# One run of probability-times-value matmuls for two head groups, and a table for the dense parts between score steps

## Chip, cores, metric

The kernel runs on one core of a Trainium2 chip. The metric is the device time of one execution in microseconds (us), as the median of several runs.

## What is computed

A parallel block on 2048 tokens of width 640: a layer norm, then sliding-window attention (32 heads of width 20, window 256) and a sigmoid-gated feed-forward of width 1536, both added to the input.

```python
scores = jnp.einsum("bhqd,bhkd->bhqk", q, k) * (Dh ** -0.5)
mask = (idx[:, None] - idx[None, :] >= 0) & (idx[:, None] - idx[None, :] < W)
p = _softmax(jnp.where(mask[None, None], scores, -1e9), axis=-1)
o = jnp.einsum("bhqk,bhkd->bhqd", p, v)
...
h = _sigmoid(g) * u                  # g = xn @ w_gate, u = xn @ w_up
xn = _layernorm(x, axis=-1)
return x + _A_ref(xn, A_wqkv, A_wo) + _B_ref(xn, B_w_gate, B_w_up, B_w_down)
```

## The kernel before, in words

The sequence is cut into four chunks c of 512 tokens. For each chunk the kernel makes the normalised, transposed input `xnT` (`g_norms`, `turn_block`), projects Q and K (`g_qk`, L292) and V (`g_v`, L318), computes gate and up (`g_gu`, L392 and L399) and at the end the down projection plus the output projection of attention (`g_out`, `down` L413, `add_wo` L420). These are the dense matmuls: 128 rows by 128 columns of weights against 512 or 320 moving columns. Each block of five of them accumulates in one of three PSUM buffers (`ps_d`) and is then read by ScalarE (the tanh of the gate, L395; the copies of K, L298, and of half of V, L325) or VectorE (`h`, L403; the copies of Q, L296, and of the other half of V; the sum with x, L424).

Q and K go through DRAM to be spread over 32-row strips: a block of Q or K is copied to `st`, stored to the scratch `sq` or `sk` (L300) and read back by `spread` (L307) into `qT` or `kT`, eight head groups of four heads each. All of these transfers are issued by SyncE (SP) in the order of the program. `spread` of Q is issued after the second K block of a chunk, `spread` of K after the first row block of V.

Attention goes in 76 steps: 16 in chunk 0 and 20 in each of the chunks 1 to 3. A step (`scores`) does 16 to 32 small matmuls (L459; 20 rows by 64 columns of weights, several in different parts of the array at once), which fill the single score buffer `ps` of four PSUM banks. ScalarE takes the exponential of all of it into a probability tile `pT` (L464, 2048 columns), and GpSimd masks parts of that (L467, up to three selects). In chunk 0 a step belongs to one head group; later a pair of groups takes five steps: two "wide" steps of the first group, one "full" step with the unmasked key blocks of both, and two wide steps of the second group.

`pv` multiplies the probabilities by V for one group (L491; 128 rows by 32 columns of weights, four heads in four column strips), accumulates in the one buffer of `ps_a` and is followed by a transpose on VectorE (L501) and, deferred to `fill.behind`, the division by the row sum (L509, L513) and a transpose to `oc` (L517). It is called two steps after the group's last score step, directly ahead of that later step's scores.

The order on TensorE is written by the recording loop (L663 to L688): for each step, first the due `pv`, then `scores`, then dense parts from a queue of generators (`Fill`), each giving the nanoseconds of TensorE that a part stands for (`MM` = 216 for a 512-column matmul). How many is set by `fill.pull(credit)`: what is left of dense work ahead of a deadline, divided by the steps left. A part is a whole block of five matmuls, or a piece of the down projection. `fill.shut` keeps the output projection of a chunk back until its last `pv` is recorded. After the loop the last chunk's down and output projection follow, with the last group's `pv` in their midst (L707). Everything is in manual order: each engine executes its instructions as they are recorded.

Of the kernel before, what the change touches and what calls it, by code (L numbers as in the profile page):

```python
# [86 lines left out]
def steps_of(c):  # L87
    if c == 0:
        return [wide_step(g, r, False) for g in range(NG) for r in range(2)]
    out = []  # L90
    for g in range(0, NG, 2):
        out += [wide_step(g, 0, True), wide_step(g, 1, True), full_step((g, g + 1)),
                wide_step(g + 1, 0, True), wide_step(g + 1, 1, True)]
    return out


# [11 lines left out]
def kernel(  # L108
# [21 lines left out]
    lnp = pool("lnp", 4)  # L130
    xtp = pool("xtp", 2)
    stp = pool("stp", 5)
    qp = pool("qp", 2)
    kp = pool("kp", 3)
    vp = pool("vp", 10)
    hp = pool("hp", 14)
    pp = pool("pp", 4)
    op = pool("op", 7)
    onp = pool("onp", 2)
    tp = pool("tp", 1)  # L140
    np_ = pool("np", 1)
    ps_a = pool("ps_a", 1, space=bass.MemoryType.PSUM)
# [142 lines left out]
    def proj_block(w, c, m):  # L285


        base = 0 if w == "q" else D
        ps = ps_d.tile([P, CW], FP32, name="pqk", tag="d")
        for d in range(DC):  # L290
            wt = wqkv[:, d, base:base + D].rearrange("p (k m) -> p m k", m=DC)
            nc.tensor.matmul(ps, lhsT=wt[:, m, :], rhs=xnT[c][:, d, :],  # L292
                             start=(d == 0), stop=(d == DC - 1))
        st = stp.tile([P, CW], BF16, name="st")
        if w == "q":
            nc.vector.tensor_copy(out=st, in_=ps)  # L296
        else:
            nc.scalar.copy(out=st, in_=ps)  # L298
        dst = scratch[w, c % 2].rearrange("(h j) s -> h j s", j=32)
        nc.sync.dma_start(out=dst[:, 4 * m:4 * m + 4, :], in_=st)  # L300

    def spread(w, c, g0, g1):

        if g0 == 0:
            qk[w, c] = (qp if w == "q" else kp).tile([P, NG, CW], BF16, name=w + "T")
        src = scratch[w, c % 2].rearrange("(g p) s -> p g s", p=P)
        nc.sync.dma_start(out=qk[w, c][:, g0:g1, :], in_=src[:, g0:g1, :])  # L307

    def new_v(c, s):
        v = vp.tile([P, H * VW + 11], BF16, name="v")  # L310
# [45 lines left out]
    def g_qk(c):  # L356
        for w in "qk":
            for m in range(DC):
                proj_block(w, c, m)
                if c == 0 and w == "q" and m == 1:  # L360
                    load_x(1)
                if w == "k" and m == 1:
                    spread("q", c, 0, NG if c else 2)
                yield 5 * MM
        if c == 0:
            spread("k", c, 0, 1)
            spread("k", c, 1, 3)
            spread("q", c, 2, 4)
            spread("k", c, 3, 4)

    def g_v(c):
        for s in range(SBC):
            new_v(c, s)
            for hf in range(2):
                proj_v(c, s, hf, nc.scalar.copy if hf else nc.vector.tensor_copy)
            if s == 0:
                spread("k", c, 0, 2)
                spread("k", c, 2, NG)
            yield 10 * 136


    ht = {}
# [5 lines left out]
    def g_gu(c, f0, f1):  # L388
        for f in range(f0, f1):
            pg = ps_d.tile([P, CW], FP32, name="pg", tag="d")  # L390
            for d in range(DC):
                nc.tensor.matmul(pg, lhsT=part(wg, d, f), rhs=xnT[c][:, d, :],  # L392
                                 start=(d == 0), stop=(d == DC - 1))
            th = tp.tile([P, CW], FP32, name="th")
            nc.scalar.activation(out=th, in_=pg, func=TANH, scale=0.5)  # L395
            yield 5 * MM
            pu = ps_d.tile([P, CW], FP32, name="pu", tag="d")
            for d in range(DC):
                nc.tensor.matmul(pu, lhsT=part(wu, d, f), rhs=xnT[c][:, d, :],  # L399
                                 start=(d == 0), stop=(d == DC - 1))  # L400
            h = hp.tile([P, CW], BF16, name="h")
            ht[c, f] = h
            nc.vector.scalar_tensor_tensor(out=h, in0=th, scalar=1.0, in1=pu, op0=ADD, op1=MULT)  # L403
            yield 5 * MM


    oc = {}
# [44 lines left out]
    def scores(c, step):  # L452
        pt = pp.tile([P, HG, PTW], BF16, name="pT")
        ps = ps_s.tile([P, HG, CW], FP32, name="ps")
        for g, hf, r, q, n, col in step["scores"]:
            kc, kb = divmod(c * SBC + r, SBC)
            key = kb * P + hf * U
            for i in range(HG):
                nc.tensor.matmul(  # L459
                    ps[hf * U:(hf + 1) * U, i, col * U:(col + n) * U],  # L460
                    lhsT=qk["k", kc][32 * i:32 * i + DH, g, key:key + U],
                    rhs=qk["q", c][32 * i:32 * i + DH, g, q * U:(q + n) * U],
                    start=True, stop=True)
        nc.scalar.activation(out=pt[:, :, 0:CW], in_=ps, func=EXP, scale=SCALE)  # L464

# [15 lines left out]
            keep(spans(step["diag"], 2, 2), spans(step["diag"], 2, 2), 2, P, 0, 1)  # L481
        return pt

    def pv(c, g, parts):
        acc = ps_a.tile([P, CW], FP32, name="acc")
        flat = [(pt, *piece[1:]) for step, pt in parts for piece in step["pv"] if piece[0] == g]
        for k, (pt, r, q, n, col) in enumerate(flat):
            v = vt[c * SBC + r]
            for i in range(HG):
                h = g * HG + i  # L490
                nc.tensor.matmul(  # L491
                    acc[32 * i:32 * i + 32, q * U:(q + n) * U],
                    lhsT=v[:, h * VW:h * VW + 32], rhs=pt[:, i, col * U:(col + n) * U],
                    start=(k == 0), stop=(k == len(flat) - 1), skip_group_check=True)
        finish_group(c, g, acc)

    on = {}

    def finish_group(c, g, acc):
        t1 = np_.tile([P, 16, 32], FP32, name="t1")  # L500
        nc.vector.transpose(out=t1.rearrange("p b r -> p (b r)"), in_=acc)  # L501
        if c < NCH - 1 or g < NG - 1:
            fill.behind.append(lambda: scale_group(c, g, t1))
        else:
            scale_group(c, g, t1)

    def scale_group(c, g, t1):
        rec = np_.tile([P, 16, 1], FP32, name="rec")
# [11 lines left out]
    class Fill:  # L520
        def __init__(self):
            self.parts = []
            self.behind = []
            self.done = set()
            self.shut = set()

        def add(self, label, gen, cost):
            self.parts.append([label, gen, cost])

        def left(self, label):  # L530

            ahead = itertools.takewhile(lambda p: p[0] != label, self.parts)
            return sum(max(p[2], 0) for p in ahead)

        def one(self):
            label, gen, _ = self.parts[0]
            try:
                cost = next(gen)
                if cost:
                    self.flush()  # L540
                self.parts[0][2] -= cost
                return cost
            except StopIteration:
                self.parts.pop(0)
                self.done.add(label)
                return 0
# [2 lines left out]
            while self.behind:  # L549
                self.behind.pop(0)()  # L550

        def pull(self, ns):
            while ns > 0 and self.parts and self.parts[0][0] not in self.shut:
                ns -= self.one()
            return ns

        def until(self, label):
            while label not in self.done and self.parts:
# [80 lines left out]
    norms2 = g_norms(2, True)  # L639
    fill.add("gu0a", g_gu(0, 0, 4), 4 * GU)  # L640
    fill.add("wd", later(load_wd), 0)
    fill.add("gu0b", mix(g_gu(0, 4, 12), g_norms(1, True), 1), 8 * GU)
    fill.add("x2", later(load_x, 2), 0)
    fill.add("wo_i", later(turn_wo), 0)
    fill.add("qk1", g_qk(1), 50 * MM)
    fill.add("v1", g_v(1), 40 * 136)
    fill.add("wo", later(load_wo), 0)
    fill.add("gu1a", mix(g_gu(1, 0, 2), norms2, 0, 2, False), 2 * GU)
    fill.add("out0", mix(g_out(0), norms2, 0, 2), OUT)
    fill.add("x3", later(load_x, 3), 0)  # L650
    fill.add("qk2", g_qk(2), 50 * MM)
    fill.add("v2", g_v(2), 40 * 136)
    fill.add("gu1b", mix(g_gu(1, 2, 12), g_norms(3, False), 10), 10 * GU)
    fill.add("out1", mix(g_out(1), g_turns(3), 1, 3), OUT)
    fill.add("qk3", g_qk(3), 50 * MM)
    fill.add("v3", g_v(3), 40 * 136)
# [5 lines left out]
    ends = {}  # L662
    for t, (c, _, step) in enumerate(todo):  # L663
        for piece in step["pv"]:
            ends[c, piece[0]] = t


    cuts = [(ends[n, NG - 1] + 2, f"out{n}") for n in range(NCH - 1)] + [(len(todo), None)]
    fill.pull(6 * 5 * MM)
    parts = {}  # L670
    credit = 0
    fill.shut = {"out0", "out1", "out2"}
    for t, (c, k, step) in enumerate(todo):
        if k == 0 and c > 0:
            fill.until(f"qk{c}")
        if k == 2 and c > 0:
            fill.until(f"v{c}")
        for group in [x for x in ends if ends[x] == t - 2]:
            fill.flush()
            pv(*group, parts.pop(group))  # L680
            if group[1] == NG - 1:
                fill.shut.discard(f"out{group[0]}")
        made = (step, scores(c, step))
        for g in dict.fromkeys(piece[0] for piece in step["pv"]):
            parts.setdefault((c, g), []).append(made)
        last, label = next(x for x in cuts if t < x[0])
        credit += fill.left(label) / (last - t)
        credit = fill.pull(credit)  # L688
    fill.pull(10 ** 9)
    fill.flush()  # L690

    c = NCH - 1
# [10 lines left out]
    for s in range(SBC):  # L703
# [1 line left out]
            ys[s, cut] = next(tiles)  # L705
            run(down(c, s, ys[s, cut], cut))
        if s == 1:  # L707
            pv(c, NG - 1, parts.pop((c, NG - 1)))

    s = SBC - 1  # L710
    cuts = (HALVES[0], (HALF, 4 * P), (4 * P, D))
# [40 lines left out]
```

The softmax here doesn't subtract the row's maximum and nothing guards it: scores larger than these inputs give would overflow.

## Time and profile before

| quantity | us |
|---|---|
| median of 5 runs | 315.88 (315.27 to 316.95) |
| the profiled execution, its own time | 316.95 |
| its span, first to last instruction | 315.2 |
| TensorE (PE) busy | 307.4 |
| ScalarE (ACT) busy | 193.2 |
| GpSimd (POOL) busy | 159.7 |
| VectorE (DVE) busy | 157.3 |
| transfers: 33.08 MB | 105 GB/s over the span |
| TensorE's granted clock | 1.000 |

The profile is of one execution. 1.75 us of its time lie around the span. In lines of the timeline, "xN" counts instructions that stand together, and the second number is from the start of the first to the modelled end of the last; the time that a group keeps TensorE is better read from its start to the start of the next group.

### The profile page before, as it was taken

How to read it: one execution, taken by the hardware profiler on the slowest of the kernel's cores; microseconds unless marked ns; L12 is line 12 of the kernel's file. 1: busy time of each engine (PE TensorE's matmuls, PEld its weight loads, DVE VectorE, ACT ScalarE, POOL GpSimd, SP SyncE). 2: the span in 40 equal slices, each digit the busy share in tenths (PEclk: the TensorE clock that was granted, in tenths of full speed). 3: DMA queues.
4: the chain of work that ended last, by engine and by line, in shares of the span. 5: the costliest groups of instructions: out<-in, count | busy, mean ns of one | idle time of the engine just before them, and what ended most of it. 6: DMA issues, size and time to landing. Idle time of an engine off the chain costs nothing.

```text
span 315.2 us, 10536 instructions
## 1 busy us (share of the span) xinstructions
PE 307.4 (98%) x4631; PEld 176.3 (56%) x4666; DVE 157.3 (50%) x313; ACT 193.2 (61%) x179; POOL 159.7 (51%) x257
## 2 busy tenths in 40 slices
PE   8899999999999999999999999999999999999996
PEld 3554444556566656644466656544456764444674
DVE  3541396663865563347953542544552433673234
ACT  4634686778765458677654457776765657777200
POOL 3000287766777537454954536355255656565300
DMA  7975999526733155600045025700000010000002
GB/s 250 374 248 186 351 376 170 212 75 202 205 72 70 44 173 167 204 4 0 2 42 90 23 88 141 231 2 2 3 2 23 23 44 2 4 2 2 1 2 83
DMA packets 34573, 33.08 MB, mean 105 GB/s; under 512 B 9920, under 2 KB 33984, under 8 KB 34496
## 3 DMA queue, kind: packets, MB, share of 16 engines
q1 hardware_dynamic: 34096, 32.14, 34.9%
q8 instruction: 36, 0.59, 0.8%
q10 hardware_dynamic: 432, 0.28, 0.3%
q14 instruction: 9, 0.07, 0.1%
HBM read 21.00 MB, written 10.26 MB: 99 GB/s over the span
## 4 chain that ended last, share of the span: by engine, by line
PE 94%; DMA 2%; ACT 1%; issue 1%; SPq 1%; DVE 0%; ACTq 0%
PE pg L392 16%; PE pu L399 16%; PE y L413 15%; PE pqk L292 14%; PE ps L459 9%; PE acc L491 8%; PE pv L318 7%; PE y L420 6%; DMA xc<-in_A_x_dram 2%; PE d L413 2%; PE d L420 1%; ACT pT L464 1%; PE acc L413 0%; SPq L178 0%; SPq L173 0%
## 5 line engine op out<-in xcount | busy, mean ns | idle before, releaser
L467 POOL TENSOR_SCALAR_AFFINE_SELECT pT<-pT 128x512 bf16<-128x512 bf16 (+2 forms) x192 | 145.5, 789 | 133.8 <-ACT pT L464 133.7
L464 ACT ACTIVATE pT<-ps 128x2048 bf16<-128x2048 f32 x76 | 142.7, 1877 | 63.7 <-PE ps L459 60.2
L403 DVE SCALAR_TENSOR_TENSOR h<-th,pu 128x512 bf16<-128x512 f32 x48 | 32.8, 684 | 53.8 <-PE pu L399 29.1
L392 PE MATMUL pg<-xnT,wg 128*128 128x512 bf16 x226 | 58.9, 380 | 0.7
L399 PE MATMUL pu<-xnT,wu 128*128 128x512 bf16 x228 | 58.0, 380 | 1.1 <-issue 0.8
L413 PE MATMUL y<-wd,h 128*128 128x320 bf16 (+1 forms) x348 | 50.2, 297 | 0.0
L292 PE MATMUL pqk<-xnT,wqkv 128*128 128x512 bf16 x191 | 45.6, 381 | 0.5
L413 PEld LDWEIGHTS <-h 128*128 128x128 bf16 x396 | 36.7, 98 | 14.3
L501 DVE STREAM_TRANSPOSE t<-acc 128x512 f32<-128x512 f32 x32 | 22.8, 713 | 34.3 <-PE acc L491 34.0
L395 ACT ACTIVATE th<-pg 128x512 f32<-128x512 f32 x48 | 28.6, 595 | 17.7 <-PE pg L392 13.1
L399 PEld LDWEIGHTS <-wu 128*128 128x128 bf16 x240 | 22.0, 98 | 25.6 <-issue 0.6
L392 PEld LDWEIGHTS <-wg 128*128 128x128 bf16 x240 | 22.0, 98 | 25.1 <-issue 0.4
L459 PE MATMUL ps<-qT,kT 20*64 20x128 bf16 (+4 forms) x1856 | 32.5, 239 | 0.1
L292 PEld LDWEIGHTS <-wqkv 128*128 128x128 bf16 x200 | 22.5, 119 | 18.0 <-issue 0.6
L459 PEld LDWEIGHTS <-kT 20*64 20x64 bf16 x1856 | 20.6, 103 | 19.1 <-issue 15.4
L424 DVE SCALAR_TENSOR_TENSOR xn<-y,xc 128x320 bf16<-128x320 f32 (+1 forms) x29 | 13.9, 484 | 29.6 <-PE y L420 29.4
L491 PEld LDWEIGHTS <-v 128*32 128x32 bf16 x1376 | 19.5, 97 | 13.6 <-issue 11.0
L491 PE MATMUL acc<-pT,v 128*32 128x64 bf16 (+3 forms) x1376 | 26.0, 223 | 0.0
L318 PE MATMUL pv<-wqkv,xnT 128*128 128x320 bf16 x160 | 23.9, 300 | 1.1 <-ACT xnT L273 1.0
L513 DVE TENSOR_TENSOR on<-t,rec 128x320 bf16<-128x320 f32 (+4 forms) x48 | 22.2, 463 | 1.1
L420 PE MATMUL y<-wo,oc 128*128 128x320 bf16 (+1 forms) x145 | 21.6, 297 | 0.1
L296 DVE CAST st<-pqk 128x512 bf16<-128x512 f32 x20 | 13.7, 691 | 12.2 <-PE pqk L292 12.2
(49 smaller groups left out, 153.3 us busy)
## 6 DMA issues: line engine op xcount, KB each, us to landing
qT<-sq SPq DMA_DIRECT2D x3, 1024.0 KB
sq<-st SPq DMA_DIRECT2D x20, 128.0 KB, 3.0
sk<-st SPq DMA_DIRECT2D x20, 128.0 KB, 3.6
out_dram<-xn SPq DMA_DIRECT2D x15, 160.0 KB, 1.8
kT<-sk SPq DMA_DIRECT2D x3, 768.0 KB, 4.9
wg<-in_B_w_gate_dram SPq DMA_DIRECT2D x2, 960.0 KB
wu<-in_B_w_up_dram SPq DMA_DIRECT2D x2, 960.0 KB
xc<-in_A_x_dram SPq DMA_DIRECT2D x3, 640.0 KB, 5.5
```

Source lines behind the costliest of these rows:

```text
L292: nc.tensor.matmul(ps, lhsT=wt[:, m, :], rhs=xnT[c][:, d, :], start=(d == 0), stop=(d == DC - 1))
L318: nc.tensor.matmul(ps[:, 0:HALF], lhsT=xnT[c][:, d, s * P:(s + 1) * P], rhs=wqkv[:, d, 2 * D + hf * HALF:2 * D + (hf + 1) * HALF], start=( ...
L392: nc.tensor.matmul(pg, lhsT=part(wg, d, f), rhs=xnT[c][:, d, :], start=(d == 0), stop=(d == DC - 1))
L395: nc.scalar.activation(out=th, in_=pg, func=TANH, scale=0.5)
L399: nc.tensor.matmul(pu, lhsT=part(wu, d, f), rhs=xnT[c][:, d, :], start=(d == 0), stop=(d == DC - 1))
L403: nc.vector.scalar_tensor_tensor(out=h, in0=th, scalar=1.0, in1=pu, op0=ADD, op1=MULT)
L413: nc.tensor.matmul(y[:, 0:cut[1] - cut[0]], lhsT=ht[c, f][:, s * P:(s + 1) * P], rhs=wd[:, f, cut[0]:cut[1]], start=(f == 0), stop=False)
L420: nc.tensor.matmul(y[:, 0:cut[1] - cut[0]], lhsT=oc[c, m][:, s * P:(s + 1) * P], rhs=wo[:, m, cut[0]:cut[1]], start=False, stop=(m == DC - 1))
L459: nc.tensor.matmul(ps[hf * U:(hf + 1) * U, i, col * U:(col + n) * U], lhsT=qk["k", kc][32 * i:32 * i + DH, g, key:key + U], rhs=qk["q", c] ...
L464: nc.scalar.activation(out=pt[:, :, 0:CW], in_=ps, func=EXP, scale=SCALE)
L467: nc.gpsimd.affine_select(out=out, in_=in_, pattern=[[0, HG], [0, n], [sign, width]], compare_op=GE, fill=0.0, base=base, channel_multipli ...
L491: nc.tensor.matmul(acc[32 * i:32 * i + 32, q * U:(q + n) * U], lhsT=v[:, h * VW:h * VW + 32], rhs=pt[:, i, col * U:(col + n) * U], start=( ...
```

## The change

Five things are changed together.

1. `pv` handles a pair of head groups in one run: the first group accumulates in a `ps_d` buffer, the second in `ps_a`. The first is transposed at once; its scaling, and the transpose and scaling of the second, go to `fill.behind`, which now gives one entry after each dense part instead of all at once. 32 runs of L491 become 16 (twice as long).
2. The full step of a pair moves from third to last of the five. `pv` comes two steps after the pair's last step in chunk 0, one step after it later (`LAG`), that is, directly after the dense parts behind the full step.
3. Five probability tiles instead of four (a pair's five tiles live until its `pv`); one `on` buffer instead of two.
4. `qT` is kept in half tiles of four groups: three of those instead of two whole ones, so that a chunk's Q comes in two transfers.
5. The dense blocks of `g_qk`, `g_v` and `g_gu` can be parted by a score step: after two matmuls of five, or after half of a row block of V. How many parts stand behind each step is given by the table `PARTS` in place of credit, deadlines and `shut`. The norms' places in the queue are adjusted to the smaller parts.

```diff
-        out += [wide_step(g, 0, True), wide_step(g, 1, True), full_step((g, g + 1)),
-                wide_step(g + 1, 0, True), wide_step(g + 1, 1, True)]
+        out += [wide_step(g, 0, True), wide_step(g, 1, True), wide_step(g + 1, 0, True),
+                wide_step(g + 1, 1, True), full_step((g, g + 1))]
...
-    qp = pool("qp", 2)
+    qp = pool("qp", 3)
-    pp = pool("pp", 4)
+    pp = pool("pp", 5)
-    onp = pool("onp", 2)
+    onp = pool("onp", 1)
...
+            if d == 1:
+                yield 2 * MM
...
-        nc.sync.dma_start(out=qk[w, c][:, g0:g1, :], in_=src[:, g0:g1, :])
+        nc.sync.dma_start(out=qk[w, c, half][:, first:first + g1 - g0, :], in_=src[:, g0:g1, :])
...
-                    spread("q", c, 0, NG if c else 2)
-                yield 5 * MM
+                    spread("q", c, 0, GH if c else 2)
+                    if c:
+                        spread("q", c, GH, NG)
+                yield 3 * MM
...
-    def pv(c, g, parts):
-        acc = ps_a.tile([P, CW], FP32, name="acc")
+    def pv(c, pair, parts):
+        accs = []
+        for g, home, tag in ((2 * pair, ps_d, "d"), (2 * pair + 1, ps_a, "acc")):
+            acc = home.tile([P, CW], FP32, name="acc", tag=tag)
...
+        first = turn_group(accs[0])
+        fill.behind += [lambda: scale_group(c, 2 * pair, first),
+                        lambda: scale_group(c, 2 * pair + 1, turn_group(accs[1]))]
...
-                if cost:
-                    self.flush()
+                if cost and self.behind:
+                    self.behind.pop(0)()
...
+        def take(self, n):
+            while n > 0 and self.parts:
+                n -= self.one() > 0
...
+    LAG = (2, 1, 1, 1)
+    PARTS = [
+        5, 4, 4, 7, 2, 4, 5, 4, 3, 4, 4, 4, 2, 5, 3, 5, 2, 4, 3, 4,
+        2, 5, 3, 6, 5, 3, 5, 7, 3, 3, 4, 10, 6, 6, 4, 4, 5, 3, 3, 3,
+        3, 3, 4, 8, 6, 4, 6, 5, 6, 6, 3, 5, 5, 5, 5, 4, 10, 3, 2, 3,
+        2, 3, 2, 3, 2, 3, 4, 4, 5, 6, 3, 4, 4, 5, 6, 1,
+    ]
+    fill.take(12)
...
-        for group in [x for x in ends if ends[x] == t - 2]:
+        for pair in [x for x in ends if ends[x] == t - LAG[x[0]]]:
             fill.flush()
-            pv(*group, parts.pop(group))
+            pv(*pair, parts.pop(pair))
...
-        credit = fill.pull(credit)
+        fill.take(PARTS[t])
...
-            pv(c, NG - 1, parts.pop((c, NG - 1)))
+            pv(c, GH - 1, parts.pop((c, GH - 1)))
+            fill.flush()
```

## The prediction

> **What bounds the kernel.** I read the page first: the busy shares, then the chain of work that ended last.
>
> ```profile
> PE 307.4 (98%) x4631; PEld 176.3 (56%) x4666; DVE 157.3 (50%) x313; ACT 193.2 (61%) x179; POOL 159.7 (51%) x257
> ...
> PE 94%; DMA 2%; ACT 1%; issue 1%; SPq 1%; DVE 0%; ACTq 0%
> ```
>
> TensorE is 98% busy and is 94% of the chain. But matmul ends are modelled, so I went on to TensorE's timeline and read starts: the time that a group keeps TensorE is its start to the next group's start. Between 26.4 us (the first gate block) and 312.4 us the starts follow each other with no gap that I can put down to a wait, but for one (below). So the time is a sum over TensorE's instructions plus some 30 us at the ends that the change leaves alone, and a gain must come from a shorter sum. Two kinds of L491 run (28 matmuls in chunk 0, 48 later):
>
> ```profile
> 72.40 0.68 PE L491 MATMUL acc<-pT,v 128*32 128x320 bf16 x28
> 73.01 0.43 PE L459 MATMUL ps<-qT,kT 20*64 20x320 bf16 x24
> 73.37 2.89 PE L318 MATMUL pv<-wqkv,xnT 128*128 128x320 bf16 x20
> ...
> 114.18 0.85 PE L491 MATMUL acc<-pT,v 128*32 128x320 bf16 x48
> 114.96 0.43 PE L459 MATMUL ps<-qT,kT 20*64 20x320 bf16 x24
> 115.32 2.35 PE L292 MATMUL pqk<-xnT,wqkv 128*128 128x512 bf16 x9
> ```
>
> A run keeps TensorE 0.61 or 0.785 us, a score group 0.36 us, whether dense work or L491 stands ahead of it.
>
> **What is removed.** Four heads stream side by side, so a run streams 18 x 64 = 1152 columns in chunk 0 and 24 x 64 = 1536 later. From the two runs: (785 - 612) / (1536 - 1152) = 0.45 ns a column, and 785 - 1536 x 0.45 = 93 ns belong to the run as such. That is the low end. The high end: a dense 512-column matmul comes every 216 ns, 0.42 ns a column; 1536 x 0.42 = 648, and 137 ns are left. Some of those are small per-matmul costs that stay, so I take 105, near the fit. The instruction order of the changed kernel has 16 runs of L491 instead of 32, all the same matmuls, the same 76 score groups, and dense work between any two steps as before. It saves 16 x 0.105 = **1.68 us** (1.49 to 2.19).
>
> A rule of the Trainium skill bears on this 93: TensorEngine Tiling (Array Packing), Key Properties, says that a change of tiling mode drains the engine. TensorE: Matmul & The Clock Gate, step 4 of its Part 2, puts a drain at some 128 cycles, by estimate 0.053 us at 2.4 GHz, and the saving by it would be 0.85 us; the trace's run-to-run fit is nearly twice that, and I keep the fit.
>
> The one wait of TensorE that I find is in the first output projection:
>
> ```profile
> 88.75 0.43 PE L459 MATMUL ps<-qT,kT 20*64 20x128 bf16 x32
> 89.11 0.99 PE L413 MATMUL y<-wd,h 128*128 128x320 bf16 x6
> 90.18 1.52 PE L420 MATMUL y<-wo,oc 128*128 128x320 bf16 x10
> ```
>
> Six matmuls of 0.136 us take 0.82, yet L420 comes after 1.07: it waits 0.26 us for `oc` of the last group of chunk 0, whose L491 ran at 85.22, 5 us ahead. In the new order that L491 stands one step after chunk 0, and the first L420 three score steps (over 8 us) later. **0.26 us** go, and nothing is late in their place there.
>
> **What is added: waits.** The order keeps TensorE's work; it changes what may be late. I went through every kind of wait that it brings nearer.
>
> 1. *Scores on the exponential of the step before (one `ps`).* At 110.45 scores start; the exponential starts at 111.08, takes 1.88 us and ends 2.51 after the scores' start. The closest steps of before are 2.61 apart and do not wait. The new order has three steps with only 15 matmuls of 0.136 behind 0.36 us of scores and 0.09 of switching: 2.49 apart. Each may wait 0.02 to 0.14. A fourth, the step behind the third K block in chunk 0, has two K copies (0.55 each) ahead of its exponential; from the scores before it to the end of that exponential before takes 5.26 (67.11 to 72.37), and the new order gives exactly that: 0 to 0.15. All four 0.06 to 0.57; I take **0.25**. What is queued behind these scores is all dense work, so such a wait is lost whole.
> 2. *PV on the exponential of the full step, now directly ahead of it.* Five of eleven such places have only 1.6 to 1.8 us of dense work. The full step's tile is used last by the first group, 20 column units (0.56 us) into the run, so it is wanted 0.36 + 1.60 + 0.56 = 2.52 after the scores' start at the tightest two, against 2.51. From 0 to 0.2 each; **0.15** for all. If the order within the run were not so, 0.56 each would come on top.
> 3. *`ps_d`, from which PV takes a buffer.* In two places of the output projections y0 and y1 hold the two others, and the next y needs y0's buffer. VectorE's sum takes 0.49 and starts 0.2 after L420 of y0 ends, which is 0.68 of TensorE time before the buffer is wanted. 0 to 0.5 each (0.5 if VectorE is in a transpose); **0.15** together. Elsewhere the buffers are read a block earlier than wanted.
> 4. *The first score step of chunk 1 on its K.* Before:
>
> ```profile
> 71.31 0.38 SPq L307 DMA_DIRECT2D qT<-sq  x1
> 71.75 2.31 SPq L300 DMA_DIRECT2D sk<-st  x3
> 79.57 0.88 SPq L307 DMA_DIRECT2D kT<-sk  x2
> ```
>
> The last K block ended at 72.46, `kT` went out at 79.57 and, at the 2.8 us that its 256 KB take, was there by 82.4; the scores came at 82.60. So this was tight already. In the new order this step comes earlier: 8 dense matmuls of 0.216 fewer lie before it (1.73), and 3 double runs less 0.105 each (3.36) stand for 7 single ones (4.28), together 2.65 us: 79.95. The last K block ends 6.8 us ahead of that, at 73.2. What must fit: two copies behind the exponential (1.2), the store (issue 0.1; shortest 2.0, median of `sk` 3.6), `kT` (2.8): 6.1 to 7.7. So a wait of 0 to 0.9 by these rows, and 3.1 if the whole 9.9 of before come again. Those 9.9 had the store behind Q's 1 MB, issued 2.1 us ahead of the last store; now Q (two issues of 0.4 on SP, done before the third K block is copied) goes out some 4 us ahead. I take **0.2**, close to the short end.
>
> Waits: 0.25 + 0.15 + 0.15 + 0.2 = **0.75 us**.
>
> **At nothing.** The fifth probability tile: ScalarE's waits for GpSimd (2.5 us in all) lie beside TensorE's work; without it the exponential would wait for PV in each pair. One `on` buffer: its reader and writer are both on VectorE, in order. Half tiles of Q: the second half's transfer waits for scores that ended 5 or more steps earlier; should they not have, SP would hold the K stores behind it, which is item 4 again. The deferred transposes: VectorE is 50% busy, and `ps_a` has five steps until it is wanted. Masks: GpSimd needs 2.3 to 2.5 us a step, steps are 2.5 or more apart, and the pair's last masked step is a whole step ahead of its PV. Split blocks: the same matmuls. The end: the last PV is 0.68 us longer instead of a run inside the loop; VectorE then has two groups to scale (some 4.3 us) behind 6 us of down projection, so L420 is not late.
>
> **Sum.** 1.68 + 0.26 - 0.75 = 1.19 us less. The profiled execution's own 316.95 (span 315.2 and 1.75 around it) would be 315.8. It is the slowest of the five; their median, 315.88, is 1.07 lower, and by the same difference the median becomes **314.7**.
>
> **Rivals.** A difference under 0.3% (0.95 us) can't be told from none here.
>
> - *The saving is eaten (0.35).* The waits come at their high ends: 0.57 + 0.4 + 1.0 + 0.9 = 2.9 against 1.94, 0.9 slower, 316.8; or about half of them come, and the time is 0 to 0.9 below. That the saving isn't there at all, because a change of the accumulator inside the run costs as much as a new run, belongs here: 315.88 + 0.75 - 0.26 = 316.4. Against it: in a score group the four heads write four banks 3 to 4 ns apart, so a new bank alone has no price.
> - *Slower, by chunk 1's K (0.13).* If the transfers from the third K store to `kT` take as long as before, 9.9 us, the first scores of chunk 1 wait 3.1 instead of 0.2, and everything behind them on TensorE with them: 314.7 + 2.9 = 317.6. It costs from a chain of 6.8 us on; from 6.8 + 1.39 = 8.2 on the whole change is slower than before, from 9.1 on by more than 0.3%. For it: the same stores, the same queue, 1 MB of Q ahead of them. Against it: that Q leaves earlier relative to them.
> - *Forecast (0.52):* 0.95 to 2.2 us faster, 313.7 to 314.9.
>
> The lower end of the range is the full saving at its high price with hardly a wait: 315.88 - 2.45 = 313.4. The upper end takes in the eaten saving, 316.5, and leaves most of the slower case out. Faster by over 0.3% 0.52, within 0.35, slower 0.13.
>
> **What would show it.** Right: 16 runs of L491, of some 1.12 and 1.47 us start to start; score groups still 0.36; no wait ahead of L420 in chunk 0; small gaps at the named steps. Wrong: a run of over 1.55 us (the switch is paid at the second group); a gap of over 1 us before the first scores of chunk 1 that ends with `kT`'s landing; gaps of TensorE released by ScalarE at many steps, which I have priced at four.

## The result, and the profile after

The changed kernel takes 316.5 us (median; 315.68 to 318.44) where the kernel before, on the same chips, takes 315.77 (315.11 to 316.95). The ratio is **1.0026, 95% interval 1.0019 to 1.0034**: 0.7 us slower. The forecast was 314.7 us, 1.2 us faster.

The page of the changed kernel (316.68 us, span 315.0), the rows that answer to the first two of before:

```profile
PE 303.4 (96%) x4629; PEld 175.4 (56%) x4666; DVE 157.5 (50%) x313; ACT 192.3 (61%) x179; POOL 159.9 (51%) x257
...
PE 82%; DVE 4%; POOL 4%; DMA 3%; ACT 3%; issue 3%; ACTq 0%; SPq 0%; DVEq 0%
```

TensorE's busy time (its ends are modelled) is 4.0 us less than before, and its share of the chain has fallen from 94% to 82%: the end is now reached through VectorE, GpSimd, ScalarE and a transfer as well. So TensorE waits, which it hardly did.

TensorE's timeline, with a run of each length of the merged L507 (L491 before), and the place in chunk 0 where the output projection came late before:

```profile
46.16 1.18 PE L507 MATMUL acc<-pT,v 128*32 128x320 bf16 x56
47.27 0.43 PE L472 MATMUL ps<-qT,kT 20*64 20x320 bf16 x24
...
88.94 1.80 PE L426 MATMUL y<-wd,h 128*128 128x320 bf16 x12
90.58 1.52 PE L433 MATMUL y<-wo,oc 128*128 128x320 bf16 x10
...
94.95 1.52 PE L507 MATMUL acc<-pT,v 128*32 128x320 bf16 x96
96.40 0.43 PE L472 MATMUL ps<-qT,kT 20*64 20x320 bf16 x24
```

A double run keeps TensorE 1.11 and 1.455 us where two single ones kept it 2 x 0.612 and 2 x 0.785: 0.115 less each. A score group still takes 0.36, and 12 matmuls of 0.136 (1.63) stand between 88.94 and 90.58: no wait ahead of the output projection.

For a balance I use the stretch from the first score group's start to the last matmul's start; how early TensorE's main work begins differs from one execution to the next, and the stretch leaves that out. Within it I take as a wait what a group's start-to-start time is above its streaming time. The streaming of the two kernels differs only in the runs of L507: the 16 double runs keep TensorE 21.90 us in all, the 32 single ones of before kept it 23.74.

| execution | first scores at | stretch | of it waits | streaming |
|---|---|---|---|---|
| before, first profile (316.95) | 32.94 | 279.23 | 1.38 | 277.85 |
| before, second profile (315.28) | 31.53 | 278.97 | 1.12 | 277.85 |
| after (316.68) | 31.43 | 280.46 | 4.45 | 276.01 |

Streaming is down by **1.84 us**; the prediction took 1.68 and gave 1.49 to 2.19. Waits are up by 3.33 from the second profile. Against that profile the stretch is 1.49 longer (the medians, whose executions begin at different times, differ by 0.73). The 1.1 us of the second profile is in pieces of 0.05 and less.

The view of the waits of the changed kernel (engine, instruction, releaser: us in total, times, longest) names the four that are new on TensorE within the stretch:

```profile
PE ps L472 <- DMA kT<-sk: 1.0, 1, 1.0
...
PE y L426 <- DVE h L416: 0.9, 1, 0.9
...
PE ps L472 <- ACT pT L477: 0.8, 1, 0.8
...
PE pu L410 <- DMA wu<-in_B_w_up_dram: 0.4, 1, 0.4
```

By start-to-start times:

| wait | where | us |
|---|---|---|
| up weights | step 3, up block 6: three matmuls from 40.08, next start 41.28 | 0.55 |
| exponential | the scores of step 8, at 56.40 | 0.83 |
| chunk 1's K | the scores of step 16, at 80.57 | 0.83 |
| last `h` of the down projection | behind step 37, at 160.51 | 1.06 |

They sum to 3.27, nearly all of the 3.33. Two of them end with transfers, one with an `h` of VectorE, and one with an exponential of ScalarE that VectorE had held up.

**The exponential.** TensorE, ScalarE and VectorE of the changed kernel around 55 us, one fence for each engine's timeline:

```profile
55.05 0.59 PE L410 MATMUL pu<-xnT,wu 128*128 128x512 bf16 x2
56.40 0.42 PE L472 MATMUL ps<-qT,kT 20*64 20x320 bf16 x16 [0.76 <-ACT pT L477]
```

```profile
53.98 0.60 ACT L406 ACTIVATE th<-pg 128x512 f32<-128x512 f32 x1 [1.34 <-DVE h L416]
54.48 1.87 ACT L477 ACTIVATE pT<-ps 128x2048 bf16<-128x2048 f32 x1
```

```profile
50.97 1.01 DVE L529 TENSOR_TENSOR on<-t,rec 128x192 bf16<-128x192 f32 x1
52.02 0.71 DVE L533 STREAM_TRANSPOSE oc<-on 128x512 bf16<-128x512 bf16 x1
52.77 0.53 DVE L529 TENSOR_TENSOR on<-t,rec 128x128 bf16<-128x128 f32 x1
53.22 0.67 DVE L416 SCALAR_TENSOR_TENSOR h<-th,pu 128x512 bf16<-128x512 f32 x1
```

Read it from the end. The scores wait for the exponential of the step before (54.48), which stands in ScalarE's order behind a `th` (53.98). That waited 1.34 us, since there is one `th` buffer and the `h` that reads it (53.22) stands in VectorE's order behind the second group's scaling. VectorE is 50% busy, but here it is full for as long as the buffers last. Two of the scalings shown ran beside selects of GpSimd and took 1.01 and 0.53 us, where the same widths took 0.36 and 0.29 with none beside them (at 155.81 and 154.74): 0.89 us more of VectorE's time. No run takes the selects away, so what the wait would be without them isn't shown.

**The last `h`.** TensorE, VectorE and GpSimd of the changed kernel:

```profile
157.96 1.66 PE L426 MATMUL y<-wd,h 128*128 128x320 bf16 x11
160.51 0.31 PE L426 MATMUL y<-wd,h 128*128 128x320 bf16 x1 [0.89 <-DVE h L416]
```

```profile
157.04 0.71 DVE L520 STREAM_TRANSPOSE t<-acc 128x512 f32<-128x512 f32 x1
...
158.07 1.06 DVE L529 TENSOR_TENSOR on<-t,rec 128x320 bf16<-128x320 f32 x1
159.17 0.71 DVE L533 STREAM_TRANSPOSE oc<-on 128x512 bf16<-128x512 bf16 x1
159.80 0.65 DVE L416 SCALAR_TENSOR_TENSOR h<-th,pu 128x512 bf16<-128x512 f32 x1
```

```profile
156.45 2.34 POOL L480 TENSOR_SCALAR_AFFINE_SELECT pT<-pT 128x512 bf16<-128x512 bf16 x3 [2.24 <-ACT pT L477]
```

Eleven of the twelve matmuls have their `h`; the twelfth's stands behind the second group's transpose and scaling, 2.76 us of VectorE. The scaling among these took 1.06 us beside the last of three selects of GpSimd; with none beside it, it takes 0.49, so 0.57 of VectorE's 2.76 come from there.

**Chunk 1's K.** TensorE and SP of the changed kernel:

```profile
79.22 0.38 PE L401 MATMUL pg<-xnT,wg 128*128 128x512 bf16 x1
80.57 0.43 PE L472 MATMUL ps<-qT,kT 20*64 20x320 bf16 x24 [0.98 <-DMA kT<-sk]
```

```profile
77.75 0.88 SPq L312 DMA_DIRECT2D kT<-sk  x2
```

The last K block ended at 72.85; its copies ended at 73.78, `kT` went out at 77.75, when the store of 73.88 had landed, and the scores started 2.82 us later. That is 7.7 us, where the working gave 6.1 to 7.7 and the order left 6.8. Of the two gate matmuls at 79.22 the trace has one record; the wait is the 1.35 to 80.57 less 2 x 0.216 and 0.09 of switching.

### The profile page after: what moved, and what is told of

Same layout as the page of the kernel before. It is cut to its first block, busy times and chain, and to the rows that moved or that the text cites. A ratio compares the mean times of both kernels' runs of the same rounds, so it can differ in the third digit from the quotient of the medians.

```text
span 315.0 us, 10530 instructions
## 1 busy us (share of the span) xinstructions
PE 303.4 (96%) x4629; PEld 175.4 (56%) x4666; DVE 157.5 (50%) x313; ACT 192.3 (61%) x179; POOL 159.9 (51%) x257
## 4 chain that ended last, share of the span: by engine, by line
PE 82%; DVE 4%; POOL 4%; DMA 3%; ACT 3%; issue 3%; ACTq 0%; SPq 0%; DVEq 0%
PE y L426 15%; PE pqk L292 13%; PE pu L410 13%; PE pg L401 13%; PE ps L472 8%; PE y L433 6%; PE acc L507 6%; PE pv L323 5%; POOL pT L480 3%; ACT pT L477 2%; PE d L426 2%; DMA sk<-st 1%; POOL rstd L259 1%; DVE h L416 1%; DMA xc<-in_A_x_dram 1%
## 5 line engine op out<-in xcount | busy, mean ns | idle before, releaser
L410 PE MATMUL pu<-xnT,wu 128*128 128x512 bf16 x225 | 59.7, 380 | 1.8 <-issue 1.0
L401 PE MATMUL pg<-xnT,wg 128*128 128x512 bf16 x228 | 60.0, 380 | 0.9 <-issue 0.5
L426 PE MATMUL y<-wd,h 128*128 128x320 bf16 (+1 forms) x348 | 51.1, 297 | 0.9 <-DVE h L416 0.9
L529 DVE TENSOR_TENSOR on<-t,rec 128x320 bf16<-128x320 f32 (+4 forms) x48 | 22.4, 467 | 1.7
L507 PE MATMUL acc<-pT,v 128*32 128x64 bf16 (+3 forms) x1376 | 23.0, 222 | 0.0
L507 PEld LDWEIGHTS <-v 128*32 128x32 bf16 x1376 | 18.6, 97 | 7.8 <-issue 3.2
L433 PEld LDWEIGHTS <-oc 128*128 128x128 bf16 x165 | 15.8, 98 | 5.9
```

What stands on the lines that cost most here:

```text
L426: nc.tensor.matmul(y[:, 0:cut[1] - cut[0]], lhsT=ht[c, f][:, s * P:(s + 1) * P], rhs=wd[:, f, cut[0]:cut[1]], start=(f == 0), stop=False)
L433: nc.tensor.matmul(y[:, 0:cut[1] - cut[0]], lhsT=oc[c, m][:, s * P:(s + 1) * P], rhs=wo[:, m, cut[0]:cut[1]], start=False, stop=(m == DC - 1))
L507: nc.tensor.matmul(acc[32 * i:32 * i + 32, q * U:(q + n) * U], lhsT=v[:, h * VW:h * VW + 32], rhs=pt[:, i, col * U:(col + n) * U], start=( ...
```

## The experiments

**Theory A**: the merged runs save what was worked out, and four waits, each with a cause of its own, take it back; what makes the late transfer or the late VectorE work earlier brings each wait's time. **Theory B**, the rival: the order has no room left, so that a wait that is taken away comes back at the next place. A further rival for the forecast was that merging itself brings the waits, whatever surrounds it. Ratios are against the kernel before, run beside each experiment (its medians there: 315.71, 315.69, 315.69, 315.64); "stretch" is as above, 280.46 after and 278.97 before.

### late: chunk 1's first scores later

Two parts more behind step 15, two fewer behind step 21.

```diff
-        5, 4, 4, 7, 2, 4, 5, 4, 3, 4, 4, 4, 2, 5, 3, 5, 2, 4, 3, 4,
-        2, 5, 3, 6, 5, 3, 5, 7, 3, 3, 4, 10, 6, 6, 4, 4, 5, 3, 3, 3,
+        5, 4, 4, 7, 2, 4, 5, 4, 3, 4, 4, 4, 2, 5, 3, 7, 2, 4, 3, 4,
+        2, 3, 3, 6, 5, 3, 5, 7, 3, 3, 4, 10, 6, 6, 4, 4, 5, 3, 3, 3,
```

> Edit: two more dense parts behind step 15 and two fewer behind step 21, so that the first scores of chunk 1 stand five matmuls (1.08 us) later in the order. Theory A: their wait for K, 0.83 us in the profile, goes, 315.7 us. Theory B: the five matmuls are missed behind step 21 or the transfer is late all the same; within 0.3 us of 316.5. If the wait were caused by the position of the K stores behind Q's transfer alone, the transfers would keep their times and only the wait would end.

Measured: 315.83, ratio 1.0004 [0.9985, 1.0022]; stretch 279.82. TensorE's timeline:

```profile
80.43 0.59 PE L410 MATMUL pu<-xnT,wu 128*128 128x512 bf16 x2
80.96 0.43 PE L472 MATMUL ps<-qT,kT 20*64 20x320 bf16 x24
```

No wait: the two parts now lie where it was. The three others stay (0.75, 0.83, 1.06). Theory A for this wait; in time the interval still meets that of the changed kernel (1.0019 to 1.0034).

### gu1: the second half of the gate and up weights ahead of chunk 0's late Q and K

```diff
             spread("k", c, 1, 3)
+            load_gu(1)
             spread("q", c, 2, 4)
...
-        for k in range(1, F // FS):
-            load_gu(k)
```

> Edit: the second half of the gate and up weights (2 x 960 KB) is asked for ahead of the Q and K of the third and fourth head groups (384 KB) instead of behind them. Theory A: the first up block of that half waits 0.55 us less, 315.9 to 316.2 us, and the run-to-run spread (315.68 to 318.44) gets smaller, as this wait depends on the time at which TensorE's work begins. Theory B, or the wait has another cause: no change, or slower by a wait of step 4 for the third group's Q.

Measured: 316.46, ratio 1.0017 [1.0, 1.0033]; stretch 279.83. The step 3 wait is gone; two small ones (0.12 and 0.21) come at step 5. The stretch is 0.63 shorter, but 0.38 of that is a shorter wait for chunk 1's K (0.45 in this execution); 0.25 are left for the weights. In time the interval can't tell it from the changed kernel, and the runs' spread (315.84 to 317.8) isn't clearly smaller, though that was expected. How long this wait is differs by execution: 0.55 after, 0.75 in `late`, 1.5 in `hold`, none in `th2`, `hold2`, `norms`, `norms3` and `flush`, none of which has this edit. So one profile without the wait doesn't show that the edit removes it; the four further profiles with the edit (below) don't have it either.

### th2: two tiles for the tanh

The tiles are bf16, so the tanh is rounded to that.

```diff
-    tp = pool("tp", 1)
+    tp = pool("tp", 2)
-            th = tp.tile([P, CW], FP32, name="th")
+            th = tp.tile([P, CW], BF16, name="th")
```

> Edit: two tanh tiles in bf16 instead of one in f32, in the same space, so that the next tanh needn't wait for the h before it. Theory A: the exponential of step 7 doesn't stand behind a tanh that waits for VectorE, 0.83 us go, 315.7 us; the 1.06 us at the first down projection stay, since there TensorE waits for h itself. Theory B: within 0.3 us of 316.5.

Measured: 316.29, ratio 1.0010 [0.9991, 1.0029]; stretch 279.38. TensorE's timeline of `th2` at this place:

```profile
55.67 0.59 PE L410 MATMUL pu<-xnT,wu 128*128 128x512 bf16 x2
56.20 0.42 PE L472 MATMUL ps<-qT,kT 20*64 20x320 bf16 x16
```

The exponential's wait at step 8 is gone, which shows the chain through the one `th` buffer; it isn't the smaller type, since `h` takes 0.69 us in both kernels. Part of it came back directly behind: 0.38 for chunk 1's `xnT`, whose transposing transfer was hidden by the wait. The two waits ahead of K and the last `h` stay (0.67 and 1.06).

### hold and hold2: the second group's transpose later

`hold` leaves the second group's entry standing through the whole of `gu1b`; `hold2` only behind step 36.

```diff
-                if cost and self.behind:
+                if cost and self.behind and not (label == "gu1b" and len(self.behind) < 2):
```

> Edit: while the gate and up blocks of chunk 1 are worked through, the second group's transpose and scaling is not taken from the deferred list; it stands behind h then, and not ahead of it. Theory A (the loss is four local waits of TensorE: 0.55 us for the second half of the up weights, 0.83 for an exponential that stands behind a late tanh, 0.83 for chunk 1's K, 1.06 for an h that VectorE reaches late): the 1.06 us at the first down projection of chunk 1 goes and nothing else changes, about 315.4 us. Theory B (the waits are symptoms of an order that has no room; one that is taken away comes back at another place): within 0.3 us of 316.5.

Measured: 317.2, ratio 1.0048 [1.0032, 1.0063]; stretch 282.03. The last `h` waits only 0.21, but the edit reached one pair further than meant: an accumulator in `ps_a` was read late, and the next run of L507 stands still in its midst for 1.35 (TensorE's timeline):

```profile
153.86 0.85 PE L507 MATMUL acc<-pT,v 128*32 128x320 bf16 x48
155.88 0.32 PE L507 MATMUL acc<-pT,v 128*32 128x320 bf16 x4 [1.17 <-DVE t L520]
```

So the test of the theories is `hold2`:

```diff
-                if cost and self.behind:
+                if cost and self.behind and not (self.held and label == "gu1b"):
...
         made = (step, scores(c, step))
+        fill.held = t == 36
```

> Edit: the deferred transpose and scaling of the last pair of chunk 1 is held back for the parts behind step 36 only, so that it stands behind the h that the first down projection of chunk 1 waits for. Theory A (local waits): the 1.06 us at that down projection go and nothing else changes, 315.4 us, and 279.4 us from the first scores to the last matmul, against 280.5 in the profile of the changed kernel. Theory B (a wait taken away comes back elsewhere): over 316.2 us, with a new wait of a similar size in the steps 37 to 41.

Measured: 316.67, ratio 1.0043 [1.0023, 1.0062]; stretch 279.84. The twelfth matmul no longer waits, and the output projection one step later does (TensorE's timeline):

```profile
161.27 0.71 PE L433 MATMUL y<-wo,oc 128*128 128x320 bf16 x4
162.93 0.99 PE L433 MATMUL y<-wo,oc 128*128 128x320 bf16 x6 [0.96 <-DVE oc L533]
```

Four matmuls of 0.136 from 161.27 end at 161.81; 1.12 are waited, as much as was taken away. That the stretch is 0.62 shorter has other reasons: in this execution the up weights were not late, and the wait for K was 0.38. Theory B at this place: with the norms there, VectorE has too much to do between steps 35 and 39, in either order.

### all2: th2, hold2, late and gu1 together

> Edit: the four mendings together (two bf16 tanh tiles, the hold behind step 36, two parts moved from step 21 to 15, the second half of the gate and up weights asked for earlier). Theory A: 0.55 + 0.83 + 0.83 + 1.06 us go, less some 0.4 for the wait for chunk 1's transposed input that stood behind one of them, some 277.6 us from the first scores to the last matmul, and 313.6 us; faster than both kernels. Theory B: no better than the best of them alone, 315.8.

Measured: 314.8, ratio 0.9970 [0.9955, 0.9985]; stretch 278.43. Faster than both kernels, between the two expectations, with the 1.13 at step 38 left.

### norms, all3, norms3: what else stands in VectorE's order there

Between 149 and 157 us VectorE also normalises chunk 3's input (four of L264; the one at 153.34 waits 1.12 for `rstd` from GpSimd). `norms` moves these to the beginning of `gu1b`:

```diff
-    fill.add("gu1b", mix(g_gu(1, 2, 12), g_norms(3, False), 20, 2), 10 * GU)
+    fill.add("gu1b", mix(g_gu(1, 2, 12), g_norms(3, False), 4, 2), 10 * GU)
```

> Edit: the norms of chunk 3 start 16 dense parts earlier in the queue of chunk 1's gate and up blocks (behind part 4 instead of 20), so that VectorE is free of them when the last pair of chunk 1 is to be scaled. The theory of local waits, as it stands now (VectorE has too much to do between that PV and the first down projection; holding the scaling back only moved the 1.06 us from h to oc): the 1.06 us go, 315.5 us, about 279.4 from the first scores to the last matmul. Rival: the norms are in the way of other blocks' h there, and as much is lost between steps 31 and 35.

Measured: 320.04, ratio 1.0142 [1.0111, 1.0172]; stretch 283.38. The last `h` no longer waits, but TensorE now stands 2.22 and 2.13 us at steps 31 and 33. VectorE and GpSimd of `norms`:

```profile
149.46 0.77 DVE L264 TENSOR_SCALAR xn<-xc,mv,rstd 128x640 bf16<-128x640 bf16 x1 [3.98 <-POOL rstd L259]
```

```profile
146.24 2.34 POOL L480 TENSOR_SCALAR_AFFINE_SELECT pT<-pT 128x512 bf16<-128x512 bf16 x3 [3.12 <-ACT pT L477]
...
148.85 0.57 POOL L259 TENSOR_TENSOR rstd<-rstd,neghalf 128x1 f32<-128x1 f32 x1
```

The `rstd` stands in GpSimd's order behind selects that wait for an exponential, VectorE stands 3.98 us for it, and the `h` behind it is late. VectorE idles for these 3.98 us, and GpSimd for 3.12 ahead of its selects; two orders meet.

`all3` is `norms` with `th2`, `late` and `gu1`:

> Edit: the changed kernel with the early norms of chunk 3, two bf16 tanh tiles, two parts moved from step 21 to 15 and the second half of the weights asked for earlier. Local waits: 278.43 us from the first scores to the last matmul (the four mendings with the hold) less the 1.13 us that the hold moved to step 38: 277.3, and 313.7 us, 2 us faster than before. Rival: 314.8 as with the hold.

Measured: 317.46, ratio 1.0053 [1.0031, 1.0075]; stretch 281.09: slower than both expectations, with 2.2, 1.0 and 0.3 us of the same kind at steps 31 and 32.

`norms3` begins between the two, with a norm at every third part:

```diff
-    fill.add("gu1b", mix(g_gu(1, 2, 12), g_norms(3, False), 20, 2), 10 * GU)
+    fill.add("gu1b", mix(g_gu(1, 2, 12), g_norms(3, False), 9, 3), 10 * GU)
```

> Edit: the norms of chunk 3 begin behind part 9 of chunk 1's gate and up blocks instead of 20 and are three parts apart instead of two. If the 1.06 us at the first down projection of chunk 1 come from VectorE having norms and two groups' scaling in the same steps, and the 2.2 us waits of the run with the norms at 4 come from norms that stand on VectorE waiting for GpSimd's rstd: neither is there, 279.4 us from the first scores to the last matmul and 315.5 us. If two groups' scaling alone overloads VectorE at steps 35 to 37: the 1.06 us stay, 316.5.

Measured: 315.47, ratio 0.9998 [0.9983, 1.0014]; stretch 279.14. TensorE's timeline of `norms3` at the first down projection of chunk 1:

```profile
158.66 1.79 PE L426 MATMUL y<-wd,h 128*128 128x320 bf16 x12
160.38 0.43 PE L472 MATMUL ps<-qT,kT 20*64 20x320 bf16 x24
```

The last `h` doesn't keep it waiting and nothing comes in its place (12 x 0.136 and 0.09 of switching are 1.72); the exponential (0.84) and K (0.82) still do. So the wait did not belong to the merged order as such: the norms and the double scaling met on VectorE. Some of the gain is GpSimd's: its selects fell otherwise, and the scaling that took 1.06 us took 0.70 here.

### all0 and all4: the three other edits without and with norms3

> Edit: three mendings (two bf16 tanh tiles, two parts moved, the weights earlier), nothing done at steps 35 to 37. 278.4 us from the first scores to the last matmul and 314.8 us, with the one wait of 1.06 us left; the difference to the run with the spread norms is what steps 35 to 37 cost.

Measured: 314.73, ratio 0.9967 [0.9954, 0.9980]; stretch 278.34, with the last `h`'s 1.05 left.

> Edit: those norms, two bf16 tanh tiles, two parts moved from step 21 to 15, the second half of the weights asked for earlier; no hold. If the four waits are local and their causes are as named: 278.43 less 1.13, 277.3 us from the first scores to the last matmul, 313.7 us. If VectorE's load at steps 35 to 37 stays the cause: 314.8.

Measured: **313.59, ratio 0.9933 [0.9921, 0.9945]**; stretch 277.29. The TensorE timeline of `all4` at the down projection's last twelve matmuls and the output projection:

```profile
157.82 1.80 PE L425 MATMUL y<-wd,h 128*128 128x320 bf16 x12
159.46 0.71 PE L432 MATMUL y<-wo,oc 128*128 128x320 bf16 x4
```

Twelve of 0.136 are 1.63 and the next start comes after 1.64: `h` isn't late. Nor is `oc` behind it: the ten matmuls of the output projection and the switching take 1.45, and the next scores start at 160.91. Waits are 277.29 - 276.01 = 1.28, 0.16 more than in the second profile of before, and the stretch is 278.97 - 277.29 = 1.68 shorter than before: the saving of 1.84 less these 0.16. Against `all0` it is 1.05 in the trace and 1.14 in the median. Theory A for the sum of the four; it beats both kernels.

### merge and merge1: the merged runs alone in the kernel before

`merge` puts the merged runs, the full step last, five probability tiles, the half tiles of Q, one `on` buffer and `LAG` into the kernel before; whole blocks, credit and deadlines stay, and `fill.behind` is given all at once.

```diff
-        out += [wide_step(g, 0, True), wide_step(g, 1, True), full_step((g, g + 1)),
-                wide_step(g + 1, 0, True), wide_step(g + 1, 1, True)]
+        out += [wide_step(g, 0, True), wide_step(g, 1, True), wide_step(g + 1, 0, True),
+                wide_step(g + 1, 1, True), full_step((g, g + 1))]
...
+    def pv(c, pair, parts):
```

> Edit: the merged PV alone, put into the kernel before: pairs in one run, the full step last, five probability tiles, half tiles of Q, but whole dense blocks, the credit in place of the table, and the deferred scaling all at once. Theory A (the merging itself is worth 1.68 us; what the change loses it loses by the table's places and by one deferred entry a part): 1.68 + 0.26 less, and 0.5 to 1 of waits for the up weights and for chunk 1's K, which stand 0.6 to 0.9 us earlier in the order; 314.5 to 314.9. Rival (the merged order itself brings the waits, whoever places the dense parts): 315.7 to 316.5.

Measured: 320.5, ratio 1.0141 [1.0114, 1.0169]; stretch 283.78, with 7.8 us of waits: far slower than either expectation. The first long one, in its TensorE timeline:

```profile
56.04 1.24 PE L396 MATMUL pg<-xnT,wg 128*128 128x512 bf16 x5 [1.34 <-DVE h L407]
```

The scores of step 7 stand at 54.27 and take 0.36, so the gate block waits 1.41 for a buffer whose `h` VectorE reaches after both groups' scaling. `merge1` gives one entry behind each block:

```diff
-                if cost:
-                    self.flush()
+                if cost and self.behind:
+                    self.behind.pop(0)()
```

> Edit: the merged PV alone in the kernel before, as in the run of 320.5 us, but with the deferred scaling given out one entry after each dense block. If the long stretch on VectorE makes the 4.8 us of that run: 1.3 us waits at h-bound blocks in chunk 0 and at the steps 35 to 37 shrink, 316.5 to 318. If the whole dense blocks and the credit make them (a block of five matmuls needs its buffer sooner behind a merged run): 319.5 or more.

Measured: 319.23, ratio 1.0109 [1.0083, 1.0134]; stretch 283.03, waits 7.0; between the two expectations. In the order of before the merged runs cost 3.5 to 4.8 us, and one entry per block mends under 1.3 of that. So the further rival holds there: merging alone brings far more waiting than it saves, and the smaller parts, the table and the dealing out are what the changed kernel owes its small loss to.

### flush: the changed kernel with the deferred work all at once

```diff
-                if cost and self.behind:
-                    self.behind.pop(0)()
+                if cost:
+                    self.flush()
```

> Edit: the changed kernel with the deferred scaling given out as before the change, all at once behind the first dense part. If VectorE's long stretch between two h is what costs (some 4.5 us for two groups in one piece, against the 2.2 us of one group before): 1.5 us or more slower than the changed kernel, 318 or over, with waits of TensorE for h or for a ps_d buffer that h frees. If deferral one by one is what brings the waits (it lets scaling run into later blocks): faster, 315.

Measured: 323.96, ratio 1.026 [1.023, 1.029]; stretch 288.06, with 12.0 us of waits, seven of them of over 0.8. In its VectorE the two groups' scaling is one block, and what stands behind it is late: TensorE's waits end with `h`, with the copy of a Q block to `st` or with a sum of the output projection. In the changed kernel one entry per part is worth 7.5 us (323.96 - 316.5).

### again: the kernel before, a second profile

No edit: a second profile of the same kernel, for the size of the chance in one profile.

> The kernel before, unchanged, for a second profile. From the first scores to the last matmul 279.2 us as in the first profile, if TensorE's order is all that counts; up to 0.5 more if its work begins 1.5 us earlier than in the first profile and the second half of the up weights is then late here as well.

Measured: 315.28, stretch 278.97. TensorE's timeline at the first output projection of chunk 0:

```profile
87.69 0.99 PE L413 MATMUL y<-wd,h 128*128 128x320 bf16 x6
88.51 1.52 PE L420 MATMUL y<-wo,oc 128*128 128x320 bf16 x10
```

Six matmuls take 0.82 here: no wait ahead of L420.

## Why the prediction was wrong

- **Removed runs: right, and a little more than taken.** 1.84 us by the starts of the runs, 0.115 a run, where the fit gave 0.093 and 0.105 was taken. `all4`, whose waits are 0.16 above those of before, is 1.68 shorter.
- **The wait of 0.26 ahead of L420: misread, and a chance.** The second profile of before doesn't have it; a wait that one execution shows was taken as a gain for all. And it wasn't for `oc`: VectorE of the kernel before wrote that of the last group from 87.90 to 88.61, 1.57 us ahead of L420 at 90.18.

```profile
87.90 0.71 DVE L517 STREAM_TRANSPOSE oc<-on 128x512 bf16<-128x512 bf16 x1
```

  L420's other operand, `wo`, comes by transfers that were issued from 80.49 on (from 79.32 in the second profile); the trace has no landing for them, so what was late there stays open.
- **"The deferred transposes: VectorE is 50% busy, and `ps_a` has five steps until it is wanted": this is the step that failed.** It looked for who waits for the accumulator and used VectorE's mean. What stands behind the scaling in VectorE's order is `h`, which frees the one `th` buffer and is itself wanted by the down projection. Priced at nothing, it cost 0.83 (`th2` removes it) and 1.06 (`norms3` removes it), 1.9 us together, as much as the whole saving. At both places VectorE's scalings were also longer beside GpSimd's selects than alone, by 0.89 and 0.57 us, which the prediction didn't price either. `flush` and `merge` show the same mechanism at its full size. My own question, what is queued behind the moved instruction, was not put to VectorE.
- **Waits for exponentials by TensorE's own pace: over-priced.** I took 0.25 for scores and 0.15 for `pv` on the full step; the named places show 0.14 and nothing I can read. The 0.15 for `ps_d` in the output projections did not come either.
- **Chunk 1's K: mechanism right, size off.** 0.2 taken, 0.83 measured, inside the 0 to 0.9 given. The store took 3.8 to land where I chose near the short end of 2.0 to 3.6. The rival's 3.1 stayed away.
- **The up weights: not seen.** With no L491 run and the same parts ahead of it, up block 6 comes earlier, and its weights had no room. 0.55 in this execution, from none to 1.5 in others.

The sum by measured terms: 0.55 + 0.83 + 0.83 + 1.06 + 0.14 = 3.41 of new waits and 1.04 in small pieces (1.12 in the second profile of before), less 1.84 saved: 3.41 - 0.08 - 1.84 = 1.49, the stretch's 1.49. The outcome is the rival "the saving is eaten", for its named reason (waits), but mostly not by the waits it listed. What stays open: how much of the 0.73 us between the medians is due to when TensorE's main work begins, since I have two profiles of before and one of after; what makes the up weights late in some executions and not in others; and the single edits `gu1` and `th2`, whose 0.6 and 1.1 us in the trace hold other waits that came out shorter, and can't be confirmed one by one by their timed intervals.

## What to carry to other kernels

Where one engine runs without a gap, an edit that bunches the work of a half-idle engine must be followed through that engine's order: list what stands behind each moved instruction, which buffer it frees, and when that is wanted, step by step; a busy share says nothing there. Grain matters: the same deferred work cost nothing visible (`all4`), 1.9 us (the changed kernel) or 7.5 us more than that (`flush`), by how it was dealt out and what stood around it. And a wait that is removed has to be looked for at the next place (`hold2`, `norms`) before its time is counted.

## What the runs showed of the hardware

- **VectorE beside GpSimd.** In the changed kernel the six 128 x 320 scalings (L529) with no GpSimd instruction beside them took 0.49 us each; of the ten with one beside them five took 0.49 too, the others 0.70, 0.70, 0.78, 0.82 and 1.06. The 192-wide ones: 0.36 alone, up to 1.01. The Trainium skill, SBUF — State Buffer, "SBUF: two separate sides", says that a VectorE instruction with two SBUF inputs and a GpSimd one that reads SBUF share a port pair that the first to start holds for its whole length. The trace agrees: in all five slow cases a select had started first, and the scaling ended 0.34 us behind that select's end, whenever that was. The 1.06 one started at 158.07; the third select ended at 158.79 (156.45 + 2.34), and the scaling at 159.13. So 0.15 of its 0.49 us lay inside the block. In three of the five cases of 0.49 a select had started first too, but ended within 0.15 us of the scaling's start.
- **Switching to the small matmuls.** In the second profile of before, the last dense matmul ahead of L491 or of scores kept TensorE 0.093 us longer than one ahead of another dense matmul, in all 76 places. It comes once a step whether a run of L491 stands between or not, so it isn't in the 1.84.
- **The start.** In the kernel before, the first scores came at 31.5 or 32.9 us in two profiles of one kernel, 1.4 us apart. A difference of 1 us between two single profiles is not a finding until the start is taken out.
